# Attention and MLP in one kernel: first tiles normalized one by one behind warming products, key sums fused in pairs, ten P slots, a recalibrated order

## The chip, the cores and the metric

The kernel runs on one core of one Trainium2 chip. The metric is the device time of one execution in microseconds (us), and lower is better. The engines are called TensorE (PE in the profile; PEld is its weight load), VectorE (DVE), ScalarE (ACT), GpSimd (POOL) and SyncE (SP, which issues the DMAs).

## The reference

The input has 2048 tokens of 1024 values. There are 32 heads of 32 dimensions, the hidden layer has 3584 columns, and everything is bf16.

```
xn = layernorm(x)
q, k, v = split(xn @ wqkv)                      # 32 heads of 32
s = softmax(q k^T / sqrt(32)) v @ wo            # no mask
m = gelu(layernorm(xn) @ w1 + b1) @ w2 + b2
out = x + s * silu(m)
```

The attention needs 32 x 2048 x 2048 exponentials. In this kernel they are 1024 ScalarE instructions on 128x1024 tiles.

## The kernel before

The kernel is written in instructions of the engines. A small list scheduler inside the kernel file (`_Plan`) decides the order of each engine when the program is built. Each operation is given an estimated duration, a priority and its dependencies; the scheduler plays the program forward with these estimates, and what comes out is the order of the program, so a change of one estimate or of one threshold can change the order of thousands of instructions.

The attention is cut into 512 units. A unit is four heads, 256 queries and 256 keys: 8 score products with 32 rows each on TensorE, two exponentials on ScalarE into a slot P, and products of P with V on TensorE. The softmax needs the sums over the keys. VectorE halves the work (PA adds the two key blocks of one unit, PB adds the PA of two units), and a product with ones on TensorE does the rest. Where VectorE would be late, the scheduler drops a sum (it is "dead"), and TensorE multiplies the unreduced tiles with ones instead.

```python
NP = 9          # P slots
NPA = 7
...             # cut: unit(u, pv), the sums of one unit
pa = dve(lambda e: e.tensor_tensor(PA[ai][:], P[pi][:, :, 0, :], P[pi][:, :, 1, :], op=ALU.add), c_b16(1024),
         [("P", pi, 0), ("P", pi, 1)], [("PA", ai)], PAPRIO)
...             # cut: ones_pair(u, pv, ...), the sum of two units
pb = dve(lambda e: e.tensor_tensor(PA[a0][:], PA[a0][:], PA[a1][:], op=ALU.add), c_b16(1024),
         [("PA", a1)], [("PA", a0)], PBPRIO)
```

MLP, projections, transposes and the first V, K and Q products are "dense" items which TensorE takes up between score products, so that ScalarE keeps having scores to work on. When the last unit's scores are done, TensorE still has products left (the last products with P, and output products with Wo, 512 columns each); these are what the kernel ends with.

The head reads tokens in 16 tiles of 128. VectorE computes statistics; GpSimd takes the power -1/2 for two tiles together and normalizes both; TensorE transposes; ScalarE copies the result out of PSUM (the memory for TensorE's results); then K (and Q for the first pair) are multiplied, and the first exponential can start.

```python
for n in range(NPR):                            # pairs of tiles
    ...                                         # cut: bn_stats, bn_aggr on VectorE for tiles 2n, 2n + 1
    pool(... lnp[:, lo:hi, 1] = pow(lnp[:, lo:hi, 0], mhalf) ...)
    pool(... lnp[:, lo:hi, 5] = lnp[:, lo:hi, 4] * lnp[:, lo:hi, 1] ...)
    for t in (lo, lo + 1):
        pool(lambda e, t=t: e.tensor_scalar(xnb[t % 4], xst[t], lnp[:, t, 1:2], lnp[:, t, 5:6],
                                            op0=ALU.mult, op1=ALU.add), 950, ...)
    pro_q += [tr_item(lo), tr_item(lo + 1), k_pair_item(n, n == 0)]
    if n >= 2:
        pro_q.append(v_item(0, n - 2, "pro"))
```

The softmax here doesn't subtract the row's maximum and nothing guards it: scores larger than these inputs give would overflow.

## Time and profile before

The median of three runs was 1067.57 us (1066.21 to 1068.18). The profiled execution has a span of 1065.3 us.

The page's first, fourth and fifth parts of the kernel before follow: busy time and share of each engine, shares of the chain of work that ended last, and the two costliest groups (output from input, shapes, count; busy us, mean ns; idle time just before them and its main cause).

```profile
PE 1022.9 (96%) x14561; PEld 645.8 (61%) x14617; DVE 947.5 (89%) x1803; ACT 1029.6 (97%) x1186; POOL 33.0 (3%) x44
ACT 89%; PE 7%; DVE 2%; POOL 1%; DMA 0%; issue 0%
...
L1016 ACT ACTIVATE P<-ps 128x1024 bf16<-128x1024 f32 x1024 | 984.0, 1211 | 10.6 <-PE ps L1007 7.6
L1022 DVE TENSOR_TENSOR PA<-P 128x1024 bf16<-128x1024 bf16 x502 | 337.4, 682 | 62.9 <-PE ps L655 36.1
```

ScalarE is the limit, with TensorE close behind it: 97% against 96%, and the chain lies on ScalarE for 89% of the span. In the trace, two 1024-wide exponentials start 904 ns apart when nothing holds the second one. (The Trainium skill, "Perfetto Trace Analysis", section "Optimizing Scalar/DVE Operations", gives ScalarE an overhead of about 51 ns on PSUM for each operation. With its 0.833 ns per element from "ScalarE: Activation LUTs", section "What ACT_TABLE_LOAD costs", that makes an estimate of 904 ns; this trace agrees.) The mean duration of 1211 ns is longer because successive instructions overlap. So durations must not be added up here; the distances between starts are used instead.

This gives a simple ledger of the span. It has the time before ScalarE's first copy, the issue time of all its instructions (904 ns each at 1024 columns, 520 at 512; 1015.0 us together), the "late starts" (each start-to-start distance minus 904 or 520), and the tail from the start of the last exponential to the end.

| | before, profiled run |
|---|---|
| before the first copy | 10.03 us |
| issue | 1015.0 us less the last instruction |
| late starts before 100 us / from 100 to 930 / after 930 | 13.31 / 9.39 / 3.18 us |
| from the last exponential's start to the end | 15.26 us |

The stretches of the same kernel as windows (stretch, length, busy us and count of PE, PEld, DVE, ACT, POOL, granted TensorE clock, DMA share, GB/s) show where ScalarE is not full:

```profile
0.00:100.00 100.00, 81.82 (x1107) 56.49 (x1109) 75.09 (x172) 79.86 (x90) 30.72 (x42) 0.98 0.54 155
100.00:930.00 830.00, 816.03 (x11783) 525.85 (x11812) 767.54 (x1432) 829.94 (x966) 0.00 (x0) 1.00 0.53 150
930.00:1066.00 136.00, 125.08 (x1686) 63.49 (x1696) 104.84 (x201) 119.81 (x133) 2.31 (x2) 0.98 0.40 124
```

In the first 100 us ScalarE is busy for 79.86 us, and between 100 and 930 it has no gap to speak of. The timeline of the head of the kernel before (start, us, engine, line, operation, count, and in brackets the idle time before it and what ended it) shows why:

```profile
7.70 2.38 POOL L796 TENSOR_SCALAR gw<-hT,lnp 128x1024 bf16<-128x1024 bf16 x2
10.03 1.02 ACT L772 ACTIVATE big<-ps 128x1024 bf16<-128x1024 bf16 x1 [7.81 <-PE ps L769]
12.28 3.60 PE L660 MATMUL ps<-big,qk 128*128 128x256 bf16 x16 [1.11 <-ACT big L772]
15.91 0.69 DVE L755 CAST qk<-ps 128x512 bf16<-128x512 f32 x1 [1.85 <-PE ps L660]
17.19 1.94 ACT L1016 ACTIVATE P<-ps 128x1024 bf16<-128x1024 f32 x2 [4.96 <-PE ps L1007]
...
48.45 1.94 ACT L1016 ACTIVATE P<-ps 128x1024 bf16<-128x1024 f32 x2 [1.94 <-PE ps L1007]
```

GpSimd needs 2.38 us for two tiles, the K and Q products take 3.60 us for 16 because TensorE's clock is still halved, and VectorE stands 1.85 us in front of the eviction. The first exponential starts at 17.19. The next seven units need keys from the other 14 tiles, so ScalarE waits several times more. Unit 7, whose first exponential starts at 48.45, is the last one that needs new tiles. One more thing matters later: the first eight units all put their scores into the same four PSUM banks (`k0 = 0 if u < NARROW` in the kernel), while the later ones go round six.

### The profile page before, as it was taken

How to read it: one execution, taken by the hardware profiler on the slowest of the kernel's cores; microseconds unless marked ns; L12 is line 12 of the kernel's file. 1: busy time of each engine (PE TensorE's matmuls, PEld its weight loads, DVE VectorE, ACT ScalarE, POOL GpSimd, SP SyncE). 2: the span in 40 equal slices, each digit the busy share in tenths (PEclk: the TensorE clock that was granted, in tenths of full speed). 3: DMA queues.
4: the chain of work that ended last, by engine and by line, in shares of the span. 5: the costliest groups of instructions: out<-in, count | busy, mean ns of one | idle time of the engine just before them, and what ended most of it. 6: DMA issues, size and time to landing. Idle time of an engine off the chain costs nothing.

```text
span 1065.3 us, 32988 instructions
## 1 busy us (share of the span) xinstructions
PE 1022.9 (96%) x14561; PEld 645.8 (61%) x14617; DVE 947.5 (89%) x1803; ACT 1029.6 (97%) x1186; POOL 33.0 (3%) x44
## 2 busy tenths in 40 slices
PE   5989999999999999999999999999999999899997
PEld 4656466656675566566665566566665666555443
DVE  7589998999989999899989998999999998968986
ACT  4899999999999999999999999999999999999994
POOL 5500000000000000000000000000000000000000
PEclk9999999999999999999999999999999999999999
DMA  9325257522764466423763466224665776562442
GB/s 267 100 68 159 66 156 200 156 75 66 204 195 127 125 169 199 114 76 101 207 197 102 128 192 195 79 76 135 196 179 169 216 216 186 161 194 78 139 128 80
DMA packets 285801, 156.55 MB, mean 147 GB/s; under 512 B 23642, under 2 KB 276570, under 8 KB 285658
## 3 DMA queue, kind: packets, MB, share of 16 engines
q1 hardware_dynamic: 285658, 154.44, 50.4%
q8 instruction: 115, 1.88, 0.7%
q14 instruction: 28, 0.23, 0.1%
HBM read 142.35 MB, written 12.06 MB: 145 GB/s over the span
## 4 chain that ended last, share of the span: by engine, by line
ACT 89%; PE 7%; DVE 2%; POOL 1%; DMA 0%; issue 0%
ACT P L1016 82%; ACT ut L888 5%; PE ps L660 4%; ACT gw L920 1%; PE ps L655 1%; DVE stats L782 1%; PE ps L1007 1%; POOL gw L796 1%; POOL lnp L810 0%; DMA hT<-in_A_x_dram 0%; DVE V L732 0%; DVE qk L760 0%; DVE mv L784 0%; DVE yT L860 0%; PE ps L769 0%
## 5 line engine op out<-in xcount | busy, mean ns | idle before, releaser
L1016 ACT ACTIVATE P<-ps 128x1024 bf16<-128x1024 f32 x1024 | 984.0, 1211 | 10.6 <-PE ps L1007 7.6
L1022 DVE TENSOR_TENSOR PA<-P 128x1024 bf16<-128x1024 bf16 x502 | 337.4, 682 | 62.9 <-PE ps L655 36.1
L660 PE MATMUL ps<-yT,w1r 128*128 128x256 bf16 x1792 | 231.9, 274 | 1.8 <-DVE yT L860 0.8
L660 PE MATMUL ps<-w2r,hT 128*128 128x256 bf16 x1792 | 229.4, 274 | 1.8 <-DVE hT L890 1.3
L660 PEld LDWEIGHTS ps<-yT,w1r 128*128 128x128 bf16 x1792 | 162.3, 98 | 56.0 <-issue 30.0
L660 PEld LDWEIGHTS ps<-w2r,hT 128*128 128x128 bf16 x1792 | 161.4, 98 | 55.1 <-issue 33.4
L655 PE MATMUL ps<-P,V 128*32 128x256 bf16 x4096 | 147.5, 276 | 1.6 <-DVE xb L880 0.7
L660 PE MATMUL ps<-big,qk 128*128 128x512 bf16 (+1 forms) x509 | 122.4, 368 | 6.1 <-ACT big L772 2.3
L1039 DVE TENSOR_TENSOR PA<-PA 128x1024 bf16<-128x1024 bf16 x182 | 123.3, 681 | 1.0
L660 PE MATMUL ps<-qk,big 128*128 128x256 bf16 (+1 forms) x723 | 121.7, 305 | 2.5 <-issue 1.6
L655 PEld LDWEIGHTS ps<-P,V 128*32 128x32 bf16 x4096 | 101.6, 97 | 26.6 <-issue 13.1
L1007 PE MATMUL ps<-qk 32*128 32x256 bf16 x2048 | 102.1, 274 | 9.8 <-ACT P L1016 8.4
L1007 PE MATMUL ps<-QKT 32*128 32x256 bf16 x2048 | 101.8, 273 | 5.5 <-ACT P L1016 4.8
L888 ACT ACTIVATE ut<-ut 128x512 f32<-128x512 f32 x112 | 92.1, 835 | 0.0
L660 PEld LDWEIGHTS ps<-qk,big 128*128 128x128 bf16 x736 | 65.5, 98 | 40.7 <-issue 15.2
L890 DVE SCALAR_TENSOR_TENSOR hT<-ut,xb 128x512 bf16<-128x512 f32 x112 | 75.4, 676 | 12.1 <-ACT ut L888 12.0
L660 PEld LDWEIGHTS ps<-big,qk 128*128 128x128 bf16 x552 | 49.0, 99 | 55.0 <-issue 15.6
L880 DVE TENSOR_TENSOR xb<-ps,b1T 128x512 bf16<-128x512 f32 x112 | 76.7, 685 | 3.3 <-PE ps L660 2.6
L886 DVE SCALAR_TENSOR_TENSOR ut<-sq,xb 128x512 f32<-128x512 bf16 x112 | 76.2, 684 | 0.7
L1007 PEld LDWEIGHTS ps<-qk 32*128 32x128 bf16 x2048 | 30.4, 92 | 75.9 <-ACT P L1016 72.9
L1007 PEld LDWEIGHTS ps<-QKT 32*128 32x128 bf16 x2048 | 30.4, 92 | 75.0 <-ACT P L1016 73.5
L655 PE MATMUL ps<-PA,ones 128*32 128x256 bf16 x1280 | 71.5, 275 | 0.0
(65 smaller groups left out, 523.2 us busy)
## 6 DMA issues: line engine op xcount, KB each, us to landing
w1r<-in_B_w_dram SPq DMA_DIRECT2D x112, 512.0 KB, 4.3
w2r<-in_B_w_dram SPq DMA_DIRECT2D x128, 448.0 KB, 4.3
qk<-in_A_wqkv_dram SPq DMA_DIRECT2D x16, 256.0 KB, 3.0
g_scratch<-gw SPq DMA_DIRECT2D x32, 128.0 KB, 3.4
o_scratch<-ot SPq DMA_DIRECT2D x56, 64.0 KB, 2.6
big<-o_scratch SPq DMA_DIRECT2D x28, 128.0 KB, 3.3
hT<-in_A_x_dram SPq DMA_DIRECT2D x10, 256.0 KB, 5.7
qk<-in_A_wqkv_dram SPq DMA_DIRECT2D x4, 512.0 KB, 3.8
```

The source lines that it names most:

```text
L655: ins = e.matmul(dst(j), lhsT=lhsT(j), rhs=rhs(j), start=start, stop=stop, tile_position=(0, 32 * j), skip_group_check=True)
L660: return e.matmul(dst, lhsT=lhsT, rhs=rhs, start=start, stop=stop, skip_group_check=True)
L782: dve(lambda e, t=t, c=c: e.bn_stats(stats[:, t, c, :], xst[t][:, c * 512:(c + 1) * 512]), 600, [XS(t)], [("st", t, c)], 1)
L796: pool(lambda e, t=t: e.tensor_scalar(xnb[t % 4], xst[t], lnp[:, t, 1:2], lnp[:, t, 5:6], op0=ALU.mult, op1=ALU.add), 950, [XS(t), ("nb_", ...
L880: dve(lambda e: e.tensor_tensor(xb_t[i3][:].rearrange("p (k t) -> p k t", k=2), bank(it.bank).rearrange("p (k t) -> p k t", k=2), b1T[:, 2 ...
L886: dve(lambda e: e.scalar_tensor_tensor(ut_t[i3][:], sq_t[p % 2][:], 1.0 / GA, xb_t[i3][:], op0=ALU.add, op1=ALU.mult), c_f32(512), [("sq", ...
L888: act(lambda e: e.activation(ut_t[i3][:], ut_t[i3][:], ACT.Tanh, scale=GC * GA), c_act(512), [("ut", i3)], [("ut", i3)], 1)
L890: dve(lambda e: e.scalar_tensor_tensor(hT[:, hs].rearrange("p k t -> p (k t)"), ut_t[i3][:], 1.0, xb_t[i3][:], op0=ALU.add, op1=ALU.mult), ...
L1007: ins = e.matmul(bank(b0[j], kk * 256, (kk + 1) * 256), lhsT=QKT[sl][32 * j:32 * j + 32, 1, kb * 128:(kb + 1) * 128], rhs=QKT[sl][32 * j:3 ...
L1016: x = act(lambda e, h=h: e.activation(P[pi][:, 2 * h:2 * h + 2].rearrange("p j k q -> p (j k q)"), ps[:, pr[h] * 1024:(pr[h] + 1) * 1024], ...
L1022: pa = dve(lambda e: e.tensor_tensor(PA[ai][:], P[pi][:, :, 0, :], P[pi][:, :, 1, :], op=ALU.add), c_b16(1024), [("P", pi, 0), ("P", pi, 1 ...
L1039: pb = dve(lambda e: e.tensor_tensor(PA[a0][:], PA[a0][:], PA[a1][:], op=ALU.add), c_b16(1024), [("PA", a1)], [("PA", a0)], PBPRIO)
```

## The change

Four things were changed together. (a) The first two tiles are normalized one by one on VectorE, with a power for each tile on GpSimd; tile 1's transposed copy is split between ScalarE and VectorE; K and Q are multiplied tile by tile. Before that, 13 products of the identity with itself keep TensorE busy, so that its clock is released when the first real product comes. (b) The key sums of two units become one VectorE instruction of 2048 columns. (c) P gets ten slots instead of nine and PA eight instead of seven; the room comes from smaller or shared scratch tiles. (d) Thresholds and estimates of the scheduler are set anew, so the order of all engines is another one.

```diff
-GRACE2 = 1200
+GRACE2 = 600
-RESERVE = 800
-GLAST = 12
-NOPA = 8
+RESERVE = 300
+GLAST = 11
+NOPA = 24
-AGE_D = 3500
-HOLD = 500
-OLAG = 0
-GRACE1 = 2500
+AGE_D = 2500
+HOLD = 400
+OLAG = 1
+GRACE1 = 8000
+PJB = 16                     # was the 14 of "(2, 14)" below; PJA 2, PJC 12, PJD 7 are unchanged
 ...
-        NP = 9
-        NPA = 7
+        NP = 10
+        NPA = 8
 ...
-        Q256, Q512 = 109.0, 216.0
+        Q256, Q512 = 110.3, 217.3
 ...
+        pro_q.append(warm_item())          # 13 products ident x ident, 512 columns
 ...
+            if n == 0:
+                for t in (0, 1):
+                    dve(... lnp[:, t:t + 1, 0] = mv[:, t:t + 1, 1] + EPS ...)
+                    pool(... lnp[:, t:t + 1, 1] = pow(lnp[:, t:t + 1, 0], mhalf[:, t:t + 1]) ...)
+                    dve(lambda e, t=t: e.tensor_scalar(xnb[t], xst[t], mv[:, t, 0:1], lnp[:, t, 1:2],
+                                                       op0=ALU.subtract, op1=ALU.mult), ...)
+                pro_q += [tr_item(0), qk_tile_item(0), tr_item(1, 0), tr_item(1, 1), qk_tile_item(1)]
+                continue
 ...
-                lo, n = (2, 14) if w == 0 else (16 + 19 * (w - 1) + 12, 7)
+                lo, n = (PJA, PJB) if w == 0 else (16 + 19 * (w - 1) + PJC, PJD)
 ...
-            o = add("PE", s_fn, 2 * Q256, TL, [("Q", sl, qb), ("K", sl, kp)], ...)
+            o = add("PE", s_fn, 235.0, TL, [("Q", sl, qb), ("K", sl, kp)], ...)
 ...
-            pa = dve(lambda e: e.tensor_tensor(PA[ai][:], P[pi][:, :, 0, :], P[pi][:, :, 1, :], op=ALU.add), c_b16(1024), ...)
+            pa = dve(lambda e: e.tensor_tensor(PA_all[:, a0:a0 + 2]...,            # in ones_pair: two units
+                                               P_all[:, p0:p0 + 2, :, 0, :]...,
+                                               P_all[:, p0:p0 + 2, :, 1, :]..., op=ALU.add), c_b16(2048), ...)
```

Cut from the diff: the scratch tiles that were moved, tokens that are now kept per half of a transposed tile, two more estimates (the mode switch of TensorE 100 to 95, ScalarE's slope 0.833 to 0.836), and lines that follow from the fused sum.

## The prediction

> **What bounds it.** ScalarE. The page gives ACT 1029.6 us of 1065.3 busy and puts 89% of the chain on it. In the timeline successive 1024-wide exponentials start 904 ns apart when nothing holds them, and a 512-wide tanh takes 520 ns. So 1024 exponentials, 144 tanh and 16 transposed copies need 1015.1 us of issue, which the change leaves alone but for half a copy (-0.4). The rest of the span is what can move: 10.0 us before ScalarE's first copy, 25.9 us of starts that came late, 14.3 us after the last exponential was issued and drained. The late starts split into 13.3 us before 100 us, 9.4 us between 100 and 930, 3.2 us after. TensorE is nearly level: 98 to 99.8% busy in each 100 us from 100 to 900 (windows).
>
> **Head.** Before: first tile's statistics at 3.54, shared normalization of tiles 0 and 1 on GpSimd (1199 ns each) ends at 10.07, copies 10.03 and 11.20, K and Q products 12.28 to 15.9 on a cold clock (213 ns apart; 109 when warm from 16.85, a full window later), first exponential 17.19. The Trainium skill, "TensorE: Matmul & The Clock Gate", Part 1, says activity of about one 3.4 us window releases the clock; this trace agrees (213 against 109 ns, clock released at 16.85 after the busy stretch from 13.44). While the cold products ran, VectorE stood in order behind their eviction (1.85 us idle before it), which delayed later statistics, so GpSimd's normalizations ended at 40.0.
>
> After: 13 products of 512 columns from about 1.4 us warm the array in idle time. Power for tile 0 about 6.3 to 6.9, [...]first copy near 8.2. Tile 1's second half copy stands on VectorE behind statistics of tile 2, whose data landed at 8.87, so near 10.1; K/Q of tile 1 to 11.3; first exponential near 13.1 (-4). GpSimd then does seven pairs at about 3.47 us each from 13.4: ends near 37.7 (-2.3). Unit 7's exponentials, before which ScalarE cannot run ahead, start near 43.2 instead of 48.45. Gain -5.3; perhaps -1 more of the waits at 52 and 68 (the latter follows a half-clock window at 64.6[...]).
>
> **Key sums.** Listing both programs: 502 sums of 1024 become 243 of 2048; pair sums go from 182 to 219; ones-products from 1360 to 1276. From 682 ns at 1024 and 418 at 512 I estimate 1.21 us per fused sum. In occupancy VectorE saves about 5 us, TensorE 21 quads of 109 ns: 2.3 us (more in the middle, as 24 opening units now skip their sums). Neither is on the chain; they only shrink the 9.4 us of small waits. Ten P slots remove some of the 2.9 us in which exponentials waited for products with P. Risk: a 1.2 us op in front of an eviction. I take -2 for the middle and end together, -3 to +2.
>
> **Tail.** Same 42 output products after the last exponential; 4 more ones-products, +0.1 us.
>
> **Sum.** -0.4 -5.3 -0.6 -2 +0.1: about 8 us, 1059.5. Range 1054.5 to 1064. Over 2% would need 21 of the some 28 us that can move.
>
> **Signs.** First exponential at 12.5 to 14; products at 109 ns or less for the first K/Q; last GpSimd normalization near 38; ScalarE solid from about 43; late starts after 100 us under 12.6 us; fused sum near 1.21 us.
>
> **What would make it wrong.** Warm products that do not release the clock, or queue in front of the transposes; VectorE's in-order evictions between statistics delaying the half copy further; the recalibrated order misjudging an engine so the late starts in the middle grow; half-clock windows falling elsewhere.

## The result, and the profile after

The changed kernel took 1061.71 us (median of 4 runs, 1060.96 to 1062.02); the kernel before took 1067.12 us beside it (4 runs). The ratio is 0.9948, with a 95% interval from 0.9931 to 0.9965. Ratios here and below are the mean time of one kernel's fast runs over the mean of the other's fast runs of the same rounds, so they are not quite the ratio of the medians. The interval lies clear of 1. The result is correct. The kernel before varies more than the changed one: of all its 35 runs here, the five with a mean granted clock of 0.992 took 1070.9 to 1071.2 us, and the 14 with 0.996 took 1066.2 to 1067.1. A ratio of means has this in it.

The page of the changed kernel, as above:

```profile
PE 1026.5 (97%) x14502; PEld 643.7 (61%) x14562; DVE 946.9 (89%) x1585; ACT 1028.9 (97%) x1186; POOL 31.2 (3%) x42
ACT 93%; PE 4%; DVE 2%; DMA 1%; issue 0%; SPq 0%; POOL 0%; POOLq 0%
...
L1067 ACT ACTIVATE P<-ps 128x1024 bf16<-128x1024 f32 x1024 | 986.8, 1243 | 5.3 <-PE ps L1058 5.3
L1087 DVE TENSOR_TENSOR PA<-P 128x2048 bf16<-128x2048 bf16 x243 | 294.7, 1215 | 25.4 <-ACT P L1067 24.1
```

A fused sum takes 1215 ns, as estimated (1.21 us). (The Trainium skill, "VectorE: DVE Perf Modes", section "The perf-mode tier table", states 1224 ns for a bf16 `tensor_tensor` of 2048 elements; this trace agrees.) VectorE's busy time is nevertheless the same, 946.9 against 947.5 us: the fused sums are busy for 42.7 us less than the single ones (294.7 against 337.4), but 37 more pair sums (219 against 182) take 24.4 us more, and with 218 fewer instructions less time is saved by one overlapping the next. The head of the changed kernel:

```profile
1.38 5.46 PE L668 MATMUL ps<-ident 128*128 128x512 bf16 x13 [1.38 <-DVE ident L710]
6.93 0.55 DVE L833 TENSOR_SCALAR gw<-hT,mv,lnp 128x1024 bf16<-128x1024 bf16 x1 [0.30 <-POOL lnp L831]
8.19 1.51 ACT L814 ACTIVATE big<-ps 128x1024 bf16<-128x1024 bf16 x2 [5.98 <-PE ps L803]
9.27 1.96 PE L668 MATMUL ps<-big,qk 128*128 128x128 bf16 x32
12.69 1.94 ACT L1067 ACTIVATE P<-ps 128x1024 bf16<-128x1024 f32 x2 [2.98 <-PE ps L1058]
16.01 1.02 ACT L814 ACTIVATE big<-ps 128x1024 bf16<-128x1024 bf16 x1 [1.38 <-PE ps L803]
20.67 1.94 ACT L814 ACTIVATE big<-ps 128x1024 bf16<-128x1024 bf16 x2 [2.46 <-PE ps L803]
...
37.00 1.20 POOL L847 TENSOR_SCALAR yT<-w2r,lnp 128x1024 bf16<-128x1024 bf16 x1
...
40.12 1.92 PE L668 MATMUL ps<-qk,big 128*128 128x256 bf16 x16 [0.23 <-ACT big L814]
...
43.20 2.36 PE L668 MATMUL ps<-qk,big 128*128 128x256 bf16 x20
43.32 1.94 ACT L1067 ACTIVATE P<-ps 128x1024 bf16<-128x1024 f32 x2 [0.50 <-PE ps L1058]
...
45.49 0.12 PEld L1058 LDWEIGHTS ps<-qk 32*128 32x128 bf16 x8 [0.21 <-ACT P L1067]
45.49 0.40 PE L1058 MATMUL ps<-qk 32*128 32x256 bf16 x8
...
45.94 14.77 ACT L1067 ACTIVATE P<-ps 128x1024 bf16<-128x1024 f32 x16 [0.68 <-PE ps L1058]
```

The opening works as meant. The 32 K and Q products of 128 columns, which are the same work as the 16 of 256 before, take 1.96 us instead of 3.60, and the first exponential starts at 12.69, which is 4.5 us earlier. But unit 7 starts at 45.94 and not at 43.2, which is only 2.5 us earlier than before: 2.0 us of the start are given back between the two. ScalarE does the same instructions there in both kernels, so this is all late starts. Those over 0.3 us are 1.67, 0.77, 0.89 and 2.15 us before (5.5 together), and 1.49, 2.58, 0.77, 0.34, 0.31, 0.46, 0.72 and 0.79 us after (7.5 together).

The first and the last window of the changed kernel:

```profile
0.00:100.00 100.00, 91.50 (x1314) 63.01 (x1318) 71.67 (x161) 82.83 (x95) 28.86 (x40) 0.98 0.56 161
...
930.00:1061.00 131.00, 120.61 (x1563) 59.85 (x1573) 106.38 (x175) 116.08 (x129) 2.31 (x2) 1.00 0.41 126
```

The granted clock of the last stretch is now 1.00 instead of 0.98. Two shorter windows of the kernel before show what had been there:

```profile
941.86:945.28 3.42, 1.13 (x20) 0.60 (x21) 2.66 (x5) 3.42 (x5) 0.00 (x0) 1.00 0.99 260
945.00:950.00 5.00, 5.00 (x93) 3.25 (x95) 1.50 (x3) 3.57 (x5) 0.00 (x0) 0.66 0.14 41
```

Before, TensorE was busy for only 1.13 us of the 3.42 us up to 945.28. The clock was then at half until 948.7, and an exponential started 1.73 us late at 949.2. After the change this is gone:

```profile
940.00:945.00 5.00, 3.77 (x103) 2.48 (x100) 3.68 (x6) 5.00 (x8) 0.00 (x0) 1.00 0.69 192
```

The two ledgers, from the profiled runs:

| | before | after | difference | predicted |
|---|---|---|---|---|
| first copy | 10.03 | 8.19 | -1.84 | |
| half copy less to issue | | | -0.38 | -0.4 |
| late starts before 100 us | 13.31 | 12.38 | -0.93 | |
| head together | | | -3.15 | -6.3 |
| late starts, 100 to 930 us | 9.39 | 8.95 | -0.44 | |
| late starts after 930 us | 3.18 | 1.76 | -1.42 | |
| middle and end together | | | -1.86 | -2 |
| tail | 15.26 | 15.19 | -0.07 | +0.1 |
| sum (span 1065.3 to 1060.2) | | | -5.08 | -8.2, stated as about 8 |

### The profile page after: what moved, and what is told of

Read it like the earlier page. It is cut to its first block, busy times and chain, and to the rows that moved or that the text cites. A ratio compares the mean times of both kernels' runs of the same rounds, so it can differ in the third digit from the quotient of the medians.

```text
span 1060.2 us, 32647 instructions
## 1 busy us (share of the span) xinstructions
PE 1026.5 (97%) x14502; PEld 643.7 (61%) x14562; DVE 946.9 (89%) x1585; ACT 1028.9 (97%) x1186; POOL 31.2 (3%) x42
## 4 chain that ended last, share of the span: by engine, by line
ACT 93%; PE 4%; DVE 2%; DMA 1%; issue 0%; SPq 0%; POOL 0%; POOLq 0%
ACT P L1067 86%; ACT ut L939 5%; PE ps L668 3%; ACT gw L971 2%; DVE stats L823 1%; DMA hT<-in_A_x_dram 1%; PE ps L663 1%; ACT big L814 0%; PE ps L1058 0%; PE ps L803 0%; DVE yT L911 0%; POOL gw L847 0%; DVE V L740 0%; DVE mv L825 0%; SPq L693 0%
## 5 line engine op out<-in xcount | busy, mean ns | idle before, releaser
L1087 DVE TENSOR_TENSOR PA<-P 128x2048 bf16<-128x2048 bf16 x243 | 294.7, 1215 | 25.4 <-ACT P L1067 24.1
L668 PE MATMUL ps<-yT,w1r 128*128 128x256 bf16 x1792 | 234.9, 275 | 2.3 <-DVE xb L931 1.1
L668 PE MATMUL ps<-w2r,hT 128*128 128x256 bf16 x1792 | 226.9, 273 | 0.3 <-DVE nv L1121 0.2
L1091 DVE TENSOR_TENSOR PA<-PA 128x1024 bf16<-128x1024 bf16 x219 | 147.7, 684 | 1.4
L663 PE MATMUL ps<-P,V 128*32 128x256 bf16 x4096 | 142.8, 274 | 0.6 <-DVE xb L931 0.4
L668 PE MATMUL ps<-big,qk 128*128 128x512 bf16 (+2 forms) x522 | 120.9, 357 | 5.7 <-issue 2.1
L663 PEld LDWEIGHTS ps<-P,V 128*32 128x32 bf16 x4096 | 97.7, 96 | 33.1 <-issue 19.6
L939 ACT ACTIVATE ut<-ut 128x512 f32<-128x512 f32 x112 | 94.5, 855 | 0.0
L663 PE MATMUL ps<-PA,ones 128*32 128x256 bf16 x1068 | 56.0, 274 | 0.3 <-DVE PA L1091 0.3
```

What stands on the lines that cost most here:

```text
L663: ins = e.matmul(dst(j), lhsT=lhsT(j), rhs=rhs(j), start=start, stop=stop, tile_position=(0, 32 * j), skip_group_check=True)
L668: return e.matmul(dst, lhsT=lhsT, rhs=rhs, start=start, stop=stop, skip_group_check=True)
L939: act(lambda e: e.activation(ut_t[i3][:], ut_t[i3][:], ACT.Tanh, scale=GC * GA), c_act(512), [("ut", i3)], [("ut", i3)], 1)
L1087: pa = dve(lambda e: e.tensor_tensor(PA_all[:, a0:a0 + 2].rearrange("p u j q -> p (u j) q"), P_all[:, p0:p0 + 2, :, 0, :].rearrange("p u j ...
```

## The experiments

Three questions were open. Which part of the change brings the gain? Why does unit 7 start later than predicted? And why are the middle and the end as good as they are? The answers proposed were: the head is limited by the GpSimd chain; or it is limited by VectorE's statistics and by the order of the products in front of the scores; the middle and end come from the fused sums; or they come from the new order. Twelve kernels were run, and every one was correct. A label such as "theory A" in a text belongs to that text.

One reading is needed for all of them. In every profile, the time from the start of the last exponential to the end is 15.2 us plus 0.217 us for each product of 512 columns beyond 51 that the built program still has on TensorE after the last score product. This holds within 0.2 us in all fourteen profiles. (The Trainium skill, "TensorE: Matmul & The Clock Gate", section "Wait — 56ns, not 53.3ns?", states about 215.7 ns from start to start for such a product on the released clock, which agrees.) The count can be read from the built program before anything runs. These chains show it, as the last lines of the chain of waits in order of time (start, us, engine, tile, line, count). First the kernel before:

```profile
1052.67 9.24 PE ps L660 x42
...
1061.93 0.70 DVE w1r L1171
```

The changed kernel:

```profile
1047.59 9.24 PE ps L668 x42
...
1056.86 0.70 DVE w1r L1221
```

And run e3 below, which has 83 of them instead of 52 and 51:

```profile
1052.85 10.74 PE ps L668 x49
...
1063.64 5.36 PE ps L668 x24
...
1069.02 0.70 DVE w1r L1210
```

In both of the first two the chain ends with 42 output products and one sum on VectorE. In e3, TensorE has 31 or 32 more to do after ScalarE is through.

In the table, "against before" is (ratio - 1) x 1067.6 us; "in the tail" is (products - 52) x 0.217 us; "elsewhere" is the difference of the two. The last two columns are therefore estimates from measured numbers. An interval reaches about 0.0015 to 0.002 to each side, which is 1.6 to 2.1 us, so a difference of that size in the last column shows nothing by itself; besides, the profiles of e6, e8 and e9 have no half-clock stretch near 58 us, and that of the changed kernel has one.

| kernel | head | sums, slots | constants | median us | ratio (95%) | products after the last score | against before | in the tail | elsewhere |
|---|---|---|---|---|---|---|---|---|---|
| before | old | old | old | 1067.12 | 1 | 52 | | | |
| after | new | new | new | 1061.71 | 0.9948 (0.9931 to 0.9965) | 51 | -5.6 | -0.2 | -5.4 |
| e1 | new, no warming | new | new | 1062.65 | 0.9954 (0.9941 to 0.9968) | 51 | -4.9 | -0.2 | -4.7 |
| e2 | new | old | old | 1062.99 | 0.9961 (0.9946 to 0.9975) | 52 | -4.2 | 0 | -4.2 |
| e3 | old | new | new | 1073.75 | 1.0056 (1.0040 to 1.0073) | 83 | +6.0 | +6.7 | -0.7 |
| e4 | new, four late tiles on VectorE | new | new | 1061.04 | 0.9944 (0.9929 to 0.9959) | 51 | -6.0 | -0.2 | -5.8 |
| e5 | new | new | old | 1068.37 | 1.0002 (0.9984 to 1.0020) | 75 | +0.2 | +5.0 | -4.8 |
| e6 | new | ten slots, single sums | new | 1063.13 | 0.9954 (0.9936 to 0.9972) | 63 | -4.9 | +2.4 | -7.3 |
| e7 | old | new | old | 1072.07 | 1.0034 (1.0015 to 1.0053) | 75 | +3.6 | +5.0 | -1.4 |
| e8 | e4 and eight filling products | new | new | 1066.20 | 0.9980 (0.9961 to 1.0000) | 78 | -2.1 | +5.6 | -7.7 |
| e9 | new | new | new but HOLD 420 | 1065.84 | 0.9982 (0.9968 to 0.9995) | 75 | -1.9 | +5.0 | -6.9 |
| e10 | old | new | new but PJB 14 | 1068.57 | 1.0006 (0.9993 to 1.0019) | 59 | +0.6 | +1.5 | -0.9 |
| e11 | new and six filling products, same order | new | new | 1061.08 | 0.9938 (0.9925 to 0.9950) | 51 | -6.6 | -0.2 | -6.4 |
| e12 | e11, tiles 2 and 3 on VectorE | new | new | 1062.34 | 0.9949 (0.9937 to 0.9962) | 51 | -5.4 | -0.2 | -5.2 |

Runs e1 to e4 ran on one chip together, with 6 runs each, and so did e5 to e8; e9 to e12 ran together with 5 runs each. The kernel before ran 11, 11 and 9 times beside them (medians 1067.09, 1068.28 and 1067.68 us).

### e1: without the warming products

```diff
-        pro_q.append(warm_item())
```

> The changed kernel without its 13 warming products, all else as changed. Theory A (the head's gain is paced by VectorE's statistics and GpSimd's normalizations, the warm array only takes away a stall of VectorE): first K/Q products at 107 to 213 ns, first exponential 2 to 3 us later than 12.69, but the last GpSimd normalization only 0.5 to 1.5 us later than 38.2 and the whole time 0.5 to 1.5 us over the changed kernel (ratio to before about 0.996). Rival B (warming is the gain of the head): the whole time grows by 3 us or more (ratio 0.9975 or more).

Measured: 1062.65 us, ratio 0.9954. The timeline of e1 shows the cold products:

```profile
9.42 3.21 PE L668 MATMUL ps<-big,qk 128*128 128x128 bf16 x32
...
13.60 1.94 ACT L1066 ACTIVATE P<-ps 128x1024 bf16<-128x1024 f32 x2 [3.75 <-PE ps L1057]
```

Products of 128 columns start 107 ns apart until the clock is released at 12.07 us, and 56 ns apart with warming, which is what the page named above states for the two clocks. But the first exponential starts only 0.9 us later than in the changed kernel (13.60 against 12.69). A delay of 2 to 3 us was expected, and that was wrong: the 32 products take only 1.25 us more. The last normalization on GpSimd (39.09 instead of 38.20) and unit 7 (46.84) are 0.9 us later too, and so is the end by the medians, as theory A had it. By ratio, the warming is worth 0.6 us, but the two intervals overlap. Rival B, that the warming is the gain of the head, is out.

### e2: the new head alone

```diff
 # the head of the changed kernel; from the kernel before:
-        NP = 10                 # and NPA 8, the fused sum
+        NP = 9                  # and NPA 7, one sum for each unit
 # all constants as before
```

> Only the new head (tiles one by one, warm products); separate key sums, nine P slots, the old constants. Theory A: the head is worth about 3 us (first copy 1.8 earlier, 1.2 us fewer late starts before 100 us) of the 5.4 us: ratio to before 0.997, late starts between 100 and 930 us about 9.4 us as before. Rival: the head's gain is all given back to waits and the rest of the change makes the 5.4 us: ratio 0.999 to 1.0.

Measured: 1062.99 us, ratio 0.9961, so -4.2 us. Its profiled run was the slowest of its six (span 1063.3 at a mean clock of 0.996; the others 1060.8 to 1061.4). The products after the last score product are the 52 of before, and the late starts between 100 and 930 us (9.77) are not smaller than before (9.39). So the head alone brings most of the gain, somewhat more than the 0.997 of theory A. The rest of the change, added on top of it, brings about 1.4 us by the two ratios, whose intervals overlap. Which part of the head brings its gain (the power for each tile, the normalization on VectorE, the split copy, the products by tile) was not separated; e1 took away the warming alone.

### e3: everything but the head

```diff
-        pro_q.append(warm_item())
 ...
-            if n == 0:
-                for t in (0, 1):
-                    ...          # the branch for tiles 0 and 1
-            pro_q += [tr_item(lo), tr_item(lo + 1), k_pair_item(n, False)]
+            pro_q += [tr_item(lo), tr_item(lo + 1), k_pair_item(n, n == 0)]
```

> All of the change but the head: fused key sums, ten P slots, recalibrated constants, with the old shared normalization and no warm products. Theory A: worth 1 to 2.5 us (ratio 0.998 to 0.999); late starts after 100 us of 10 to 11.5 us against 12.6 before. Rival: 4 us or more (ratio below 0.9965).

Measured: 1073.75 us, ratio 1.0056, slower by 6.0 us; both expectations had it faster. The tail is 22.10 us instead of 15.26; that is 6.8 us more, as the chain above shows. Its late starts are 15.41 us before 100 us (2.1 more than before), 8.92 in the middle (0.5 less) and 1.80 after 930 (1.4 less). So the same sums, slots and constants that help slightly on the new head cost 6 us on the old one, and they cost it at the very end, a millisecond away from the head. The reason is the order: the scheduler starts from another state and gets rid of fewer output products before the scores run out.

### e4: the late tiles on VectorE

```diff
             for t in (lo, lo + 1):
+                if t in (12, 13, 14, 15):
+                    dve(lambda e, t=t: e.tensor_scalar(xnb[t % 4], xst[t], lnp[:, t, 1:2], lnp[:, t, 5:6],
+                                                       op0=ALU.mult, op1=ALU.add), 470, ...)
+                    continue
                 pool(...)
```

> The changed kernel with the normalizations of tiles 12 to 15 on VectorE instead of GpSimd. If GpSimd's chain paces the head from 24 to 38 us: the last normalization near 35 instead of 38.2, unit 7's exponentials near 44 instead of 45.94, whole time 1 to 2.5 us below the changed kernel (ratio to before about 0.993). If ScalarE or VectorE already paces it, no change (ratio 0.995), or slower.

Measured: 1061.04 us, ratio 0.9944, not to be told from the changed kernel's. GpSimd's last normalization ends at 30.69 instead of 38.20. The last four, now on VectorE, start at 33.5 to 36.7 and take about half a microsecond each, so the last of all ends about 1 us earlier than in the changed kernel (37.2; near 35 was expected). Unit 7 starts at 45.62 instead of 45.94, but the first exponential is earlier by as much (12.40 against 12.69), and the waits in between are the same ones of the same size (0.73 and 0.79 us in front of the last two units). So unit 7 does not follow the end of the normalizations in this range. This speaks against the prediction's own step, which derived 43.2 us from that end; the step is tested here for 1 us, not for more.

### e5: the old constants

```diff
-GRACE2 = 600                    # and likewise RESERVE, GLAST, NOPA, AGE_D, HOLD, OLAG, GRACE1, PJB,
+GRACE2 = 1200                   # Q256, Q512, the mode switch, the score's and ScalarE's estimates
```

> The changed kernel with the old scheduling constants (new head, fused key sums, ten P slots kept). If the constants alone are needed to make fused sums fit the order: slower than head only (ratio 0.997 or more, a longer tail after the last exponential than 15.2 us, as the run with the rest alone had 22). If the order of TensorE is merely sensitive to any edit: about the changed kernel, 0.9945 to 0.9965, tail 15.2.

Measured: 1068.37 us, ratio 1.0002: the whole gain is gone. The head is as in the changed kernel (first exponential 12.63, unit 7 at 45.94). The tail is 20.27 us, because 75 products are left. So the fused sums and ten slots under the old constants cost here what the head had gained; the constants bring the output products out of the tail.

### e6: single sums under the new constants

```diff
-            pa = dve(... two units, 2048 columns ...)
+            pa = dve(lambda e: e.tensor_tensor(PA[ai][:], P[pi][:, :, 0, :], P[pi][:, :, 1, :], op=ALU.add), c_b16(1024), ...)
```

> The changed kernel with one key sum per unit again (ten slots, eight sum buffers, new constants, new head). If fusing is off the critical path, as predicted: within 1 us of the changed kernel (ratio 0.994 to 0.996), VectorE busy 5 to 20 us more. If fusing pays on the chain: 0.997 or more, late starts between 100 and 930 us of 10 us or more.

Measured: 1063.13 us, ratio 0.9954. The first line of e6's page, the engines:

```profile
PE 1032.9 (97%) x14554; PEld 643.1 (61%) x14554; DVE 964.8 (91%) x1830; ACT 1028.8 (97%) x1186; POOL 31.2 (3%) x42
```

VectorE is busy for 17.9 us more than in the changed kernel, so fusing does save time on it. But the late starts in the middle are 9.11 us against 8.95, and after 930 us they are 1.52 against 1.76. VectorE's 17.9 us are off the critical path. What e6 loses is in the tail, where it has 12 more products (17.8 us against 15.19). The fused sum by itself shows no gain that can be kept apart from the order.

### e7: fused sums and slots alone

```diff
 # e3, with all constants as before
```

> Fused sums and ten slots on the old head with the old constants: the run with the rest alone, less its constants. If the new constants made that run's 22 us tail: tail 15.2, ratio 0.998 to 1.000. If the fused sums made it: tail of 20 us or more, ratio 1.004 or more.

Measured: 1072.07 us, ratio 1.0034, slower by 3.6 us, with 75 products left and a tail of 20.27 us. So the long tail doesn't need the new constants either (the ratio expected for that was 1.004 or more). The late starts (12.98, 8.92 and 2.25 us) are together 1.7 us less than before. In e7, e5, e2 and the kernel before, which all have the old constants, TensorE runs a stretch at half clock near 945 us. In none of the ten profiles with new constants does it.

### e8: filling products and late tiles

```diff
 # e4, and after the first scaling of the MLP's input:
+            if c == 0:
+                wm = _Item("mlp")
+                for _ in range(8):
+                    chunk(wm, lambda e, b: full(e, bank(b), ident[:], ...), Q512, [("ident",)])
+                mq.append(wm)
```

> The run with tiles 12 to 15 normalized on VectorE, plus eight filler products of 512 columns in the gap of TensorE at 55 to 57 us, ahead of the first feed-forward products. If idle TensorE there brings on the half-clock window at 57.6 to 61.1 (ScalarE late by 1.1 us at 61.6): no half-clock window near 60 in any run, 0.5 to 1.2 us below the changed kernel (ratio 0.9935 to 0.9945). If not: no gain over it, or the 1.7 us of filler shows as a loss.

Measured: 1066.20 us, ratio 0.9980. The aim was to keep TensorE's clock from being halved near 58 us. The mean clock is 1.00 in five of six runs and 0.999 in the sixth, but the scheduler counts the filling products, so the order changes, 78 products are left and the tail is 21.01 us. The filling cost 5.8 us in the tail. This was a second lesson in the order, not a test of the clock.

### e9: one threshold moved by 20

```diff
-HOLD = 400
+HOLD = 420
```

> The changed kernel with one scheduler constant moved from 400 to 420, no instruction added or removed. Its listing has 75 products of 512 columns after the last score products where the changed kernel has 51. Theory C (the order decides how much of TensorE's work is left when ScalarE ends, and each product left costs 217 ns): tail after the last exponential 15.2 + 24 x 0.217 = 20.4 us, whole time about 5.2 us over the changed kernel, ratio to before 0.9985 to 1.0005. Rival (contents and waits decide, the order is a detail): 0.994 to 0.996.

Measured: 1065.84 us, ratio 0.9982. A change of 5% in one threshold gives back 3.6 us of the 5.6 (by the two ratios). Head and middle are no worse (first exponential 12.27, late starts 11.08, 9.03 and 1.71 us). The tail is 20.37 us. The last lines of its chain:

```profile
1046.18 10.74 PE ps L668 x49
...
1056.97 3.63 PE ps L668 x16
```

So the tail is a property of the order as a whole, and the changed kernel sits on a good one. The ratio is a little under the range that was expected (0.9985 to 1.0005): the tail grew by 5.18 us, as expected, but the late starts in the head were 1.3 us less than in the changed kernel, whose profile has the half-clock stretch. (The text on record says that no instruction is added or removed. That is not quite so: in the new order other sums are dropped, and the built program has 225 pair sums instead of 219 and 24 products with ones less.) The author also built 90 sets of constants near the changed kernel's without running them, and counted 51 products after the last score product in only 20 of them, 57 to 89 in the others.

### e10: everything but the head, one constant back

```diff
 # e3, and
-PJB = 16
+PJB = 14
```

> The run with the rest alone (old head, fused sums, ten slots, new constants) with one constant put back from 16 to 14, which leaves 59 products after the last score products instead of 83. Theory C: tail 15.2 + 8 x 0.217 = 16.9 us instead of 22.1, about 5 us faster than the run with the rest alone, ratio to before 0.999 to 1.002. Rival (fused sums do not suit the old head): 1.004 or more.

Measured: 1068.57 us, ratio 1.0006. With 59 products left, the tail is 16.9 us instead of the 22.10 of e3, and the time is that of the kernel before. This settles e3: its loss was mostly the tail, and without most of it the rest of the change is neither good nor bad for the old head.

### e11: filling products that leave the order alone

```diff
 # the changed kernel, and after the first scaling of the MLP's input:
+                def fill(e, b):
+                    for _ in range(6):
+                        ins = full(e, bank(b), ident[:], ident[:].unsqueeze(1).to_broadcast([128, 4, 128]), True, True)
+                    return ins
+                chunk(wm, fill, 1, [("ident",)])      # estimate 1 ns: the scheduler takes no notice
-PJA = 2
+PJA = 3                                               # these two count items, one of which is new
-PJC = 12
+PJC = 13
```

> The changed kernel with six filler products of 512 columns at about 55.6 us, weightless to the scheduler and its counts set off by one, so that the listing of TensorE is otherwise that of the changed kernel (51 products after the last score products). If idle TensorE at 54 to 57 us brings on the half-clock window near 58 to 61: mean clock 1.0 in nearly all runs, tail 15.2, 0.6 to 1 us below the changed kernel's 1061.7 (ratio 0.9935 to 0.9945). If not, clock 0.998 in most runs and no gain.

The order of TensorE is that of the changed kernel but for the six products. In the changed kernel, TensorE's half-clock stretch from 57.6 to 61.1 us follows this window:

```profile
54.23:57.65 3.42, 2.16 (x26) 1.00 (x25) 3.18 (x9) 3.42 (x5) 0.00 (x0) 1.00 0.07 22
```

In e11 the same window is full, and the timeline shows what fills it:

```profile
54.23:57.65 3.42, 3.29 (x31) 1.43 (x31) 3.21 (x8) 3.14 (x4) 0.00 (x0) 1.00 0.06 19
...
55.30 1.47 PE L668 MATMUL ps<-ident 128*128 128x512 bf16 x6
56.70 0.40 PE L1067 MATMUL ps<-qk 32*128 32x256 bf16 x8
```

Measured: 1061.08 us (1060.99 to 1061.43), ratio 0.9938 with an interval of 0.9925 to 0.9950. The mean clock was 1.00 in all five runs; in the changed kernel it was 0.998 in three of four. The wait of 1.12 us at 61.6 is gone, and a new one of 0.43 us at 57.1 has come, because a score product now stands behind the filling. That is worth about 0.7 us. The ratios differ by 1.1 us, but their intervals overlap. e11 has the lowest ratio of all that were run; it is clearly faster than the kernel before, and probably faster than the changed kernel. The clock is better told by all runs with this order of TensorE: without the filling (changed kernel, e1, e4) it was 1.00 in 8 of 16, with it (e11, e12) in 10 of 10.

### e12: the early tiles on VectorE as well

```diff
 # e11, and
+                if t in (2, 3):
+                    dve(lambda e, t=t: e.tensor_scalar(xnb[t % 4], xst[t], ...), 470, ...)
+                    continue
```

> The run before this one, with tiles 2 and 3 normalized on VectorE as well (51 products after the last score products again). ScalarE's idle time at 14.6 to 16.0 and 18.2 to 20.7 is the largest left in the head. If GpSimd's 2.4 us for these tiles make it: copies of tile 2 near 14.8 instead of 16.0, 0.5 to 1.5 us below the run before (ratio about 0.993). If VectorE's statistics, full from 10 to 23 us, make it: the wait moves to 20 to 24 us and the time stays, within 0.5 us.

Measured: 1062.34 us, ratio 0.9949, 1.3 us slower than e11 beside it. A time 0.5 to 1.5 us below e11 was expected if GpSimd makes the waits, and one within 0.5 us of it if VectorE does, so both sizes were missed. The timeline of e12 shows the two large waits at their old size:

```profile
14.21 0.53 DVE L848 TENSOR_SCALAR gw<-hT,lnp 128x1024 bf16<-128x1024 bf16 x1
...
15.46 1.94 ACT L814 ACTIVATE big<-ps 128x1024 bf16<-128x1024 bf16 x2 [1.38 <-PE ps L803]
...
19.85 1.94 ACT L814 ACTIVATE big<-ps 128x1024 bf16<-128x1024 bf16 x2 [2.46 <-PE ps L803]
```

Tiles 2 and 3 are normalized in 0.53 us each on VectorE, and GpSimd is free for tiles 4 and 5, yet ScalarE waits 1.38 and 2.46 us as in the changed kernel. The windows of e12 say why:

```profile
10.00:20.00 10.00, 7.81 (x97) 6.35 (x95) 10.00 (x27) 4.03 (x5) 4.17 (x6) 1.00 1.09 359
20.00:30.00 10.00, 8.47 (x101) 6.77 (x98) 10.00 (x27) 7.92 (x9) 8.43 (x11) 1.00 0.47 107
```

VectorE is busy for all of both stretches (in the changed kernel for 9.93 and 10.00 us). In the changed kernel, its statistics instructions alone take 7.95 and 7.08 us of the two stretches. So work that is moved onto it comes back as waits further on (1.33 us at 29.6, and 1.29 us instead of 0.72 before the last unit but one), which fits the account that the statistics pace the head. But VectorE's busy time is not all its own work. (The Trainium skill, "Trainium Architecture — The Big Picture", section "What this means for kernel authors", says that VectorE and GpSimd contend for a shared port pair, as a lock; this trace agrees.) In the changed kernel an addition of 128x2 values on VectorE took 0.72 us from 23.18 on, until 0.02 us after the end of a normalization on GpSimd, and 0.14 to 0.19 us where GpSimd normalized nothing or was within 0.2 us of its end.

## Why the prediction was right or wrong

The predicted time was 1059.5 us with a range of 1054.5 to 1064; the measured one is 1061.71. The sign and the range were right. The time was 2.2 us above the predicted one; of a gain of about 8 us, 5.1 us came by the profiles and 5.6 by the ratio.

**What bounds the kernel: right.** Until its last exponential starts, ScalarE at 904 ns per exponential is the limit in all fourteen profiles: its late starts are only 22 to 26 us of each. (That the ledger's sum gives the difference of the two spans, -5.08 us of -5.1, shows nothing: it does so by its construction.)

**The opening: right.** The clock was released in time: products of 128 columns start 56 ns apart instead of 107 in e1. The first exponential came at 12.69 (13.1 predicted), and GpSimd's last normalization ended at 38.20 (37.7 predicted).

**"Unit 7's exponentials, before which ScalarE cannot run ahead, start near 43.2 instead of 48.45": wrong in size.** This is the term that failed. It was 45.94, so -2.5 us instead of -5.3. The prediction put unit 7 5.5 us after the end of GpSimd's last normalization. It was 7.7 us after it (and 8.4 in the kernel before), because ScalarE, and not GpSimd, was then the one behind. At 38.20 ScalarE had just begun the second exponential of unit 4, and two copies and units 5 and 6 came before unit 7: seven slots of 904 ns. It also waited 0.72 and 0.79 us for the score products of units 6 and 7. These write the banks that the unit before has just filled, so they have to wait until its second exponential has read them. That one ended at 42.82 and 45.26, and the products started at 42.87 and 45.49 (the latter also stood behind V products, the last of which started at 45.29). Unit 8 has other banks, and its products started at 47.24, before the last exponential of unit 7 ended at 47.88. In all fourteen profiles unit 7's products start after the end of unit 6's second exponential, and unit 8's before the end of unit 7's. No run gave the first units more banks, so what that would save is not known. e4 took four tiles off GpSimd and ended the last normalization about 1 us earlier, and both waits stayed (0.73 and 0.79 us), as they must if ScalarE's own exponentials set them.

The rest of what was given back lies earlier, in the two large waits near 16 and 21 us (1.49 and 2.58 us). e12 showed that they did not go away when GpSimd was relieved, while VectorE was full. The first exponential came 4.5 us earlier, but VectorE's last statistics instruction ended only 1.3 us earlier (32.95 instead of 34.29). That VectorE's statistics pace the head fits both runs. That a shorter chain of statistics would give the 2.0 us back was not tried, and both e4 and e12 gave VectorE more work, so GpSimd is not excluded as a second limit near 16 and 21 us.

**"-0.4" for the half copy: counted twice.** The half copy lies before unit 7, so it is already in the start of unit 7. With 2.7 us for unit 7 and 0.4 for this, the head's shortfall of 3.15 us is accounted for (6.3 predicted). The third term, -0.6 for later waits in the head, came out at -0.64 (3.15 - 2.51); but the waiting at the half-clock stretch, which it counted on in part, was about as long as before (1.28 us at 68.5 before, 1.12 us at 61.6 after).

**"I take -2 for the middle and end together": right in sum, wrong in its reason.** It was -1.86, and that the sum fits is luck. The prediction put it down to lighter VectorE and TensorE work and to ten slots. But VectorE became lighter by 0.5 us and not by 5, and only 0.44 us of the gain lies in the middle. The other 1.42 lies after 930 us. There the kernel before has a wait of 1.73 us after the half-clock stretch near 945 us, which all four profiles with old constants have and none of the ten with new ones. That the stretch is the cause is not shown: e5 and e7 have it too, and their late starts after 930 us are 2.15 and 2.25 us, against 3.18 before and 1.76 after. e6 shows that 17.9 us of VectorE time are worth at most some tenths in the late starts. The effect of ten slots was not tried by itself and stays open.

**The tail: right (+0.1 predicted, -0.07 measured), with a risk that it did not see.** The number was read from the built program. What was missing was the knowledge that another order can leave a much longer tail: e3, e5, e7, e8 and e9 left 75 to 83 products instead of 51 and lost 5 to 7 us, up to all of what the head had gained. The gain of the new constants that these runs show is in the tail: they keep the new sums from lengthening the tail on this head (e5 against after: 5.1 us of tail).

**Half-clock stretches: named as a risk, and they did fall elsewhere.** How far they are a cause is shown only in part. e11 filled the gap in front of one, and the clock stayed at 1.00 in all of its five runs and in all of e12's. But e6, without filling, ran at 1.00 in five of six runs, and e4 in four of six, so that one profile with full clock proves little; the count over all runs under e11 speaks for the filling.

## What to carry to other kernels

When two engines are nearly level (here 97% and 96%) and the order is fixed when the program is built, count in the built program what is left for the second one when the first one ends, for every variant, before any time is believed: here each product more cost 0.217 us, and a threshold moved by 5% cost 24 of them. A part of a change that is tested under another order is another experiment, so compare parts after taking the tail away. And an earlier start is worth only what the next engine in the chain can follow: 4.5 us at the first exponential were 2.5 us at the last unit that needs new tiles, while VectorE was already full and ScalarE itself was behind.

## What the Trainium skill lacked or had wrong

- "TensorE: Matmul & The Clock Gate", Part 1: its table says that the clock is halved after at least one idle window of about 3.4 us. Here it was halved after windows in which TensorE was busy for 1.13 of 3.42 us (before, up to 945.28) and 2.16 of 3.42 us (after, up to 57.65), so, if the windows are those that end where the clock changes (these changes lie whole multiples of 3.413 us apart in the traces), an idle window is not needed. What the page lacks is the share of busy time below which a window counts. The runs do not give it either: other such windows with TensorE 55 to 75% busy were not followed by half clock, and the one before 57.65 was 63% busy. The length of the window, 3413 ns, and the two rates agree with these traces.
- No page has the duration of `pow` on GpSimd. Here it took 0.56 and 0.84 us for one column of 128 rows, 0.70 us for two, and 2.95 us for 16. Nor has one GpSimd's time for the normalization of a 128x1024 bf16 tile (`tensor_scalar` with two per-row scalars): 1.20 us, against 0.55 us on VectorE.
- No page has the duration of VectorE's statistics instruction (BATCH_NORM_STATS2), which fills most of VectorE's time in the head here: 0.67 us for 128x512 bf16, four of them for two tiles.
